# Attention, max-of-three and gated feed-forward on one core: last product's splits and sums moved to VectorE, its loads issued earlier, wo's sums in four steps in a row

## The chip, the cores and the metric

One core of a Trainium2 chip runs the whole program. The metric is the device time of one execution in microseconds; the median of the runs counts. TensorE is called PE in the rows, VectorE DVE, ScalarE ACT, GpSimd POOL, and SyncE, whose queue issues the DMAs, SP.

## What is computed

```python
scores = cap * tanh(q @ k.T / sqrt(64) / cap)        # 4 batches, 12 heads, 448 tokens, 64 wide
x   = softmax(scores) @ v                            # put together: 1792 tokens x 768
h   = maximum(maximum(x @ w1, x @ w2), x @ w3)       # 768 x 768 each
y   = h @ moe_w_out                                  # 1792 x 768
g   = silu(y @ w_gate) * (y @ w_val)                 # 1792 x 1536
out = g @ moe2_w_out                                 # 1792 x 768, float32
```

The weights arrive as 64-bit floats and are turned into float32 on the chip.

## The kernel before, in words

Every float32 matrix product is done in three: an operand is split into a high part (a copy that TensorE reads at full rate) and a low part (the operand less the high part), and high x high, high x low and low x high are summed in PSUM. Splitting (`parts_of`, L549 to L554) takes ScalarE one copy (L551) and another engine one subtraction (L554).

The change touches the end of the program. Gate and value come from 12 stages, c = 0 to 11 (`NF2`), each for 128 columns of both weights. A stage holds 14 products (`product`, L914 to L955): seven products of sums and differences in the manner of Strassen, in place of eight, for each of two token halves, p = 0 and 1. Its weights' seven operands (names o, made of A11, S3, S1, S2, A12, S4, A22) are cut in the stage before (`ops_steps`, L807 to L842): sums on GpSimd (L827), high parts on ScalarE, low parts on VectorE and two on GpSimd. VectorE adds each product's PSUM bank to tiles ct, qn and kn (L936 to L953; there are eight banks), ScalarE takes the silu (L947, L954), GpSimd multiplies (L950, L955), and the result goes to DRAM, to gd, by a store (`store`, L902 to L904). Stores wait in a list; a product sends all but the newest.

In between, the next weights are converted step by step (`convert`, L509 to L546): L527 on ScalarE, L531 to L538 on VectorE, L541 on GpSimd. Their tiles raw have two buffers. In stages 2 to 7 each stage also sums a piece of the last weight, wo, which lies converted in DRAM (wod): `sums_of_wo` (L490 to L507) loads it into a raw buffer, makes four differences on VectorE (L496), the fourth followed by a store to wsd (L500). These are four steps, at products 7, 9, 11 and 13 of the stage.

The last product, g by wo, is again of seven products, over pairs r of token blocks of 128 (7 pairs, gr holds what is loaded of gd; A11 and A12 are the two halves of a pair's first block, A21 and A22 of its second). `part` (L1045 to L1082) is one product of 18 matmuls; its list `todo` takes pairs 0 and 1 in turn, product by product, then pairs 2 to 6 one after another. `cut(i)` makes the operand of part i: a sum of blocks for S3 and S2 on VectorE, for S1 and S4 on GpSimd (L1026), then two half splits, the first half's low part on VectorE, the second's on GpSimd (`half_ops`, L958). It stands four parts ahead of its part. `split_wo` splits wo's 21 pieces (wo0 to wo20, three for each of the seven products), every third on GpSimd, and `fetch_wo` then loads the piece three further on; they share three buffers. Stage 11 takes the second token half first, since pairs 0 and 1 lie there.

Nothing is scheduled by a planner: each engine takes its instructions in the order in which the code issues them, and waits at the first one that is not ready. SP does likewise with loads and stores. The steps hang on the products of a stage in the table `at`.

Of the kernel before, what the change touches and what calls it, by code (L numbers as in the profile page):

```python
# [10 lines left out]
F32R = mybir.dt.float32r  # L11
# [3 lines left out]
ALU = mybir.AluOpType  # L15
# [93 lines left out]
def program(ctx, tc, tensors, shared, general):  # L109

    nc = tc.nc
# [6 lines left out]
    P = 128  # L118
# [533 lines left out]
    with tc.manual_schedule():  # L652
# [249 lines left out]
        def store():  # L902
            dst, src = stores.pop(0)
            nc.sync.dma_start(out=dst, in_=src)  # L904
# [9 lines left out]
        def product(c, p, n):  # L914
# [5 lines left out]
            for kk in range(3):  # L920
                k3 = slice(kk * P, (kk + 1) * P)
                for j, (s0, s1) in enumerate(((0, 0), (0, 1), (1, 0))):
# [1 line left out]
                        ps, a[:, s0, k3], m[:, kk, s1],  # L924
                        start=kk == 0 and j == 0, stop=kk == 2 and j == 2,
                    )
            while len(stores) > 1:
                store()
            add = nc.vector.tensor_add
            t = tmp.setdefault((c, p), {})  # L930
# [24 lines left out]
                nc.gpsimd.tensor_tensor(t[2], t[2], t[1], op=ALU.mult)  # L955
                stores.append((gd[:, c, (2 * p + 1) * S : (2 * p + 2) * S], t[2]))

        half_ops = (nc.vector, nc.gpsimd)  # L958
        OPS = "A11 S3 S1 S2 A12 S4 A22".split()
        WITH = "B11 T3 T1 T2 B21 B22 T4".split()  # L960
        flat0 = yo0.rearrange("p n k x s -> p (n k x s)")
# [22 lines left out]
        def split_wo():  # L984
            i = done_pieces[1]
            if i < len(pieces):
                done_pieces[1] += 1
                x, k = pieces[i]
                t = wo_c[x][:, k : k + 2]
                parts_of(t[:, :, 0], t[:, :, 1], wot.pop(i), nc.scalar, half_ops[i % 3 == 2])  # L990
                fetch_wo()

        blocks = [*range(T // P // 2, T // P), *range(T // P // 2)]
# [14 lines left out]
        def fetch_g(r, half=None):  # L1008
            c = slice(0, NF2) if half is None else slice(half * NHALF, (half + 1) * NHALF)
            for x in range(2):  # L1010
                s = blocks[2 * r + x]
                nc.sync.dma_start(out=gr[r, x][:, c], in_=gd[:, c, s * P : (s + 1) * P])

        def cut(i):
            if i >= len(todo):
                return
            r, n = todo[i]
            a11, a12, a21, a22 = (
                gr[r, x][:, y * NHALF : (y + 1) * NHALF].rearrange("p c t -> p (c t)")
                for x in range(2)  # L1020
                for y in range(2)
            )
            ve, pool_ = nc.vector, nc.gpsimd

            def add(eng, out_, x0, x1, op=ALU.subtract):
                eng.tensor_tensor(out_, x0, x1, op=op)  # L1026
                return out_

            x = OPS[n]
            if x == "S3":  # L1030
                src = add(ve, a11, a11, a21)
            elif x == "S1":
                src = add(pool_, a21, a21, a22, ALU.add)
            elif x == "S2":
                src = add(ve, a11, a22, a11)
            elif x == "S4":
                src = add(pool_, a12, a12, a11)
            else:
                src = dict(A11=a11, A12=a12, A22=a22)[x]
            for y in range(2):  # L1040
                t = wp.tile([P, 2, HW], F32R, tag="w", name=f"g{r}_{x}_{y}")
                parts_of(t[:, 0], t[:, 1], src[:, y * HW : (y + 1) * HW], nc.scalar, half_ops[y])
                ga.setdefault((r, n), []).append(t)

        def part(r, n):  # L1045
# [52 lines left out]
        for c in range(NF2):  # L1098
            at = {}
            if c + 1 < NF2:  # L1100
                for i in (0, 1, 2, 3, 3, 4, 5, 6) if c else (2, 3, 4, 5):
                    at.setdefault(i, []).append(convert_part)
                if 0 <= c + 1 - SUMS_AT < NHALF:
                    for i in (7, 9, 11, 13):
                        at.setdefault(i, []).append(convert_part)
                for i, step in enumerate(ops_steps(c + 1)):
                    at.setdefault(7 + i, []).append(step)
            both = [(n, p) for n in range(7) for p in range(2)]
            if c == 0:
                both.sort(key=lambda x: x[1])  # L1110
                for i, step in enumerate(y_steps):
                    at.setdefault(i, []).insert(0, step)
                at.setdefault(6, []).append(open_ct)
            if c == NF2 - 1:
                both.sort(key=lambda x: -x[1])
                at.setdefault(6, []).append(open_wo)
                at.setdefault(0, []).append(lambda: (open_g(0), fetch_g(0, 0)))
                for i in range(3):
                    at.setdefault(2 + i, []).append(fetch_wo)
                at.setdefault(8, []).append(lambda: ([store() for _ in [*stores]], cut(0)))  # L1120
                for i in (7, 7, 8, 9, 10, 11, 13):
                    at.setdefault(i, []).append(split_wo)
                at.setdefault(9, []).append(lambda: (fetch_g(0, 1), open_g(1), fetch_g(1, 0)))
                at.setdefault(10, []).append(lambda: (fetch_g(1, 1), cut(1)))
                at.setdefault(12, []).append(lambda: cut(2))
            for i, (n, p) in enumerate(both):
                product(c, p, n)
                for step in at.get(i, ()):
                    step()
# [3 lines left out]
        while stores:  # L1133
            store()
        cut(3)
        for i, (r, n) in enumerate(todo):
            part(r, n)
            if r < 2:
                split_wo()
                if i % 2:  # L1140
                    split_wo()
            cut(i + 4)
            if i + 4 < len(todo) and todo[i + 4][1] == 6 and todo[i + 4][0] + 2 < NPR:
                open_g(todo[i + 4][0] + 2)
                fetch_g(todo[i + 4][0] + 2)
# [25 lines left out]
```

## Time and profile before

| | before |
|---|---|
| median of 3 runs | 1103.56 us (1102.81 to 1104.5) |
| the profiled execution | 1102.74 us, of it span 1100.9 us |
| TensorE matmul busy | 1056.5 us, 96% of the span |
| VectorE busy | 762.0 us, 69% |
| GpSimd busy | 704.9 us, 64% |
| ScalarE busy | 535.9 us, 49% |
| mean granted TensorE clock | 0.987 |
| stages 0 to 11 | 614.5 to 923.8 us of the span |
| last product | from 923.8 us |

The span is the trace's own time from first to last instruction. Busy time says which engine has most work, not which one is waited for: that is read from the timeline, where a bracket behind a row gives the engine's idle time before it and what ended it. The granted clock is TensorE's as a share of full speed.

### The profile page before, as it was taken

To read this page: it belongs to the slowest core of one execution; us is meant where nothing else is said; L and a number is where in the kernel's file an instruction comes from. 1 tells how busy PE (TensorE), PEld (TensorE's weight loads), DVE (VectorE), ACT (ScalarE), POOL (GpSimd) and SP (SyncE) were. 2 spreads that over 40 slices of the span, in tenths; PEclk is the share of its full clock that TensorE was granted. 3 is DMA by queue.
4 is the path that set the end of the run, shared out by engine and by line. 5 is a ranking of instruction groups with operands and counts; after the bars stand their busy time and mean duration, and the time that the engine had idled before them with its cause. 6 is when DMAs were issued, how large, how long until landed. Compare 5 with 4: busy or idle time off the path is not lost. (4 is left out here: it accounts for less than half of the span.)

```text
span 1100.9 us, 15124 instructions
## 1 busy us (share of the span) xinstructions
PE 1056.5 (96%) x5354; PEld 914.8 (83%) x5354; DVE 762.0 (69%) x986; ACT 535.9 (49%) x842; POOL 704.9 (64%) x586
## 2 busy tenths in 40 slices
PE   8987999999999999999999999999999998799998
PEld 5533778888888888999998999999888998689998
DVE  4666898957777678767446977777777774675543
ACT  6855668867766674344435533222222333433321
POOL 1355998787887779998354356555555663676542
PEclk9989899999999999999999999999999998999999
DMA  6655445433434423433322023444443337473411
GB/s 150 164 143 127 116 112 149 119 92 113 135 99 117 123 70 121 136 119 114 100 71 83 9 83 120 149 149 148 148 149 120 108 96 232 131 223 107 130 65 40
DMA packets 165077, 131.42 MB, mean 119 GB/s; under 512 B 72832, under 2 KB 159616, under 8 KB 164992
## 3 DMA queue, kind: packets, MB, share of 16 engines
q1 hardware_dynamic: 162992, 129.91, 39.7%
q8 instruction: 44, 0.72, 0.3%
q10 hardware_dynamic: 2000, 0.46, 0.2%
q14 instruction: 41, 0.34, 0.1%
HBM read 98.70 MB, written 31.54 MB: 118 GB/s over the span
## 5 line engine op out<-in xcount | busy, mean ns | idle before, releaser
L600 PE MATMUL ps_h<-x,ws 128*128 128x448 f32 x1296 | 287.9, 368 | 0.5 <-DVE ht L626 0.5
L600 PEld LDWEIGHTS ps_h<-x,ws 128*128 128x128 f32 x1296 | 239.0, 188 | 35.2 <-issue 18.0
L554 POOL TENSOR_TENSOR ws<-w,ws 128x384 fp32r<-128x384 f32 x144 | 179.9, 1258 | 12.9 <-ACT ws L551 5.3
L541 POOL TENSOR_TENSOR t<-t,raw 128x768 uint32<-128x768 uint32 x42 | 82.9, 1974 | 114.2 <-DVE raw L538 104.6
L259 DVE TENSOR_TENSOR el<-e,eh 128x896 fp32r<-128x896 f32 x64 | 87.4, 1368 | 43.0 <-ACT eh L258 34.4
L241 ACT ACTIVATE e<-sc,four 128x896 f32<-128x896 f32 x96 | 87.2, 908 | 32.9 <-PE sc L235 32.7
L249 ACT ACTIVATE e<-e,four 128x896 f32<-128x896 f32 x96 | 99.5, 1037 | 0.8
L923 PE MATMUL ps_g<-yo,o_S 128*128 128x448 f32 x432 | 95.2, 364 | 4.5 <-DVE ct L943 3.4
L600 PE MATMUL ps_y<-ha,ws 128*128 128x448 f32 x432 | 89.4, 368 | 3.4 <-DVE ha L554 1.4
L923 PEld LDWEIGHTS ps_g<-yo,o_S 128*128 128x128 f32 x432 | 80.3, 187 | 13.0 <-DVE ct L943 4.5
L600 PEld LDWEIGHTS ps_y<-ha,ws 128*128 128x128 f32 x432 | 82.1, 191 | 10.7 <-DVE ha L554 2.0
L284 PE MATMUL pv<-eh,vs 128*128 128x448 f32 (+1 forms) x256 | 76.6, 380 | 1.4 <-POOL vs L185 1.4
L553 POOL TENSOR_SCALAR ws<-w 128x384 fp32r<-128x384 f32 x90 | 76.5, 850 | 0.0
L923 PE MATMUL ps_g<-yo,o_A 128*128 128x448 f32 x324 | 70.3, 362 | 0.0
L551 ACT ACTIVATE g_S<-gr 128x384 fp32r<-128x384 f32 x56 | 26.3, 517 | 81.1 <-POOL gr L1026 42.1
L527 ACT ACTIVATE t<-raw 128x768 f32<-128x768 f32 x42 | 37.6, 895 | 56.8 <-DMA raw<-in_moe_w_val_dram 46.3
L923 PEld LDWEIGHTS ps_g<-yo,o_A 128*128 128x128 f32 x324 | 60.7, 187 | 4.1
L531 DVE TENSOR_SCALAR t<-t 128x768 f32<-128x768 f32 x42 | 35.8, 853 | 37.2 <-ACT t L527 37.2
L554 POOL TENSOR_TENSOR g_S<-gr,g_S 128x384 fp32r<-128x384 f32 x28 | 28.7, 1025 | 51.2 <-ACT g_S L551 49.0
L284 PE MATMUL pv<-e,vp 128*128 128x448 f32 (+1 forms) x128 | 54.1, 608 | 5.9 <-DMA vp<-in_v_dram 4.4
L541 POOL TENSOR_TENSOR w<-w,raw 128x768 uint32<-128x768 uint32 x18 | 36.2, 2014 | 32.9 <-DVE raw L538 32.9
L258 ACT ACTIVATE eh<-e 128x896 fp32r<-128x896 f32 x64 | 55.0, 860 | 2.6 <-ACT e L249 0.6
(156 smaller groups left out, 2239.3 us busy)
## 6 DMA issues: line engine op xcount, KB each, us to landing
raw<-in_moe_w_dram SPq DMA_DIRECT2D x18, 768.0 KB, 4.9
raw<-in_moe_w_out_dram SPq DMA_DIRECT2D x18, 768.0 KB, 4.8
raw<-in_moe_w_gate_dram SPq DMA_DIRECT2D x12, 768.0 KB, 4.8
raw<-in_moe_w_val_dram SPq DMA_DIRECT2D x12, 768.0 KB, 4.5
gr<-gd SPq DMA_DIRECT2D x10, 768.0 KB, 6.9
rb<-rd SPq DMA_DIRECT2D x48, 112.0 KB, 3.1
h<-ht SPq DMA_DIRECT2D x24, 224.0 KB, 2.0
hr<-h SPq DMA_DIRECT2D x24, 224.0 KB, 2.8
```

What stands on the lines that cost most here:

```text
L241: nc.scalar.activation(ee[n][:, :w], ps[:, :w, :S], AF.Tanh, scale=qsc)
L249: nc.scalar.activation(t, t, AF.Exp, bias=ncap, scale=acap)
L258: nc.scalar.activation(hi, t, AF.Copy)
L259: nc.vector.tensor_sub(lo, t, f(hi))
L284: nc.tensor.matmul(pv[g][j][:, :S], a, m, start=c == 0 and x == 0, stop=c == 3 and x == len(ops) - 1,)
L527: nc.scalar.activation(f(t), high.bitcast(F32), AF.Abs)
L531: nc.vector.tensor_scalar(f(t), f(t), F64_LEAST, F64_MOST, ALU.max, ALU.min)
L541: nc.gpsimd.tensor_tensor(t, t, low, op=ALU.add)
L553: copier.tensor_scalar(hi, src, 1.0, 1.0, ALU.mult, ALU.mult)
L554: subtracter.tensor_tensor(lo, src, f(hi), op=ALU.subtract)
L600: nc.tensor.matmul(ps, a, m, start=kk == 0 and n == 0, stop=kk == NK - 1 and n == 2)
L923: nc.tensor.matmul(ps, a[:, s0, k3], m[:, kk, s1], start=kk == 0 and j == 0, stop=kk == 2 and j == 2,)
```

## The change

Four things are changed. The steps of wo's sums in stages 2 to 7 hang on products 7, 8, 9 and 10. In the last product all half splits, all wo pieces and all sums are VectorE's; the sums are no longer made in `cut` but in `pre`, which is issued one product earlier. The first load of pair 0 (its first column half) moves from stage 11 to product 7 of stage 10, the first of pair 1 from product 9 to product 6 of stage 11, and the loads of the second halves follow at products 8 and 9. From stage 10 on up to four stores may wait in the list, until product 8 of stage 11 sends them all.

```diff
-            while len(stores) > 1:
+            while len(stores) > (1 if c < NF2 - 2 else 4):
                 store()
...
-        half_ops = (nc.vector, nc.gpsimd)
...
-                parts_of(t[:, :, 0], t[:, :, 1], wot.pop(i), nc.scalar, half_ops[i % 3 == 2])
+                parts_of(t[:, :, 0], t[:, :, 1], wot.pop(i), nc.scalar, nc.vector)
...
+        PLACE = dict(A11=0, S3=0, S1=2, S2=0, A12=1, S4=1, A22=3)
+        MADE = dict(S3=(0, 2), S1=(2, 3), S2=(3, 0), S4=(1, 0))
+
+        def pre(i):
+            if i < len(todo) and OPS[todo[i][1]] in MADE:
+                r, n = todo[i]
+                a, x = blocks_of(r), OPS[n]
+                x0, x1 = MADE[x]
+                op = ALU.add if x == "S1" else ALU.subtract
+                nc.vector.tensor_tensor(a[PLACE[x]], a[x0], a[x1], op=op)
...
-            x = OPS[n]
-            if x == "S3":
-                src = add(ve, a11, a11, a21)
-            elif x == "S1":
-                src = add(pool_, a21, a21, a22, ALU.add)
-            elif x == "S2":
-                src = add(ve, a11, a22, a11)
-            elif x == "S4":
-                src = add(pool_, a12, a12, a11)
-            else:
-                src = dict(A11=a11, A12=a12, A22=a22)[x]
+            src = blocks_of(r)[PLACE[OPS[n]]]
...
-                parts_of(t[:, 0], t[:, 1], src[:, y * HW : (y + 1) * HW], nc.scalar, half_ops[y])
+                parts_of(t[:, 0], t[:, 1], src[:, y * HW : (y + 1) * HW], nc.scalar, nc.vector)
...
-                    for i in (7, 9, 11, 13):
+                    for i in (7, 8, 9, 10):
                         at.setdefault(i, []).append(convert_part)
...
-                at.setdefault(0, []).append(lambda: (open_g(0), fetch_g(0, 0)))
...
-                at.setdefault(8, []).append(lambda: ([store() for _ in [*stores]], cut(0)))
+                at.setdefault(6, []).append(lambda: (open_g(1), fetch_g(1, 0)))
+                at.setdefault(8, []).append(lambda: ([store() for _ in [*stores]], fetch_g(0, 1)))
+                at.setdefault(9, []).append(lambda: fetch_g(1, 1))
...
-                at.setdefault(9, []).append(lambda: (fetch_g(0, 1), open_g(1), fetch_g(1, 0)))
-                at.setdefault(10, []).append(lambda: (fetch_g(1, 1), cut(1)))
-                at.setdefault(12, []).append(lambda: cut(2))
+                at.setdefault(8, []).append(lambda: cut(0))
+                at.setdefault(10, []).append(lambda: (cut(1), pre(2)))
+                at.setdefault(12, []).append(lambda: (cut(2), pre(3)))
+            if c == NF2 - 2:
+                at.setdefault(7, []).append(lambda: (open_g(0), fetch_g(0, 0)))
...
         cut(3)
+        pre(4)
         for i, (r, n) in enumerate(todo):
...
             cut(i + 4)
+            pre(i + 5)
```

What this does to the order of the instructions is seen at three places. The first is VectorE's queue in the second half of stage 7 (raw119 is the piece of wo that is summed, L554 are low parts of stage 8's weights, L946 to L953 the additions of products). Before:

```order
L554 TENSOR_TENSOR o8_S3_7754<-t94_7647,o8_S3_7754 128x384
L946 TENSOR_TENSOR ct7_1_0_7661<-ps_g7_1_4_7773,ct7_1_0_7661 128x448
L496 TENSOR_TENSOR raw119_7694<-raw119_7694 128x384
L949 TENSOR_TENSOR kn0_62<-ps_g7_0_5_7790,kn0_62 128x448
L554 TENSOR_TENSOR o8_S2_7753<-t94_7647,o8_S2_7753 128x384
L949 TENSOR_TENSOR kn1_63<-ps_g7_1_5_7806,kn1_63 128x448
L496 TENSOR_TENSOR raw119_7694<-raw119_7694 128x384
L554 TENSOR_TENSOR o8_A12_7804<-t94_7647,o8_A12_7804 128x384
L953 TENSOR_TENSOR ct7_0_1_7675<-ps_g7_0_6_7823,ct7_0_1_7675 128x448
L554 TENSOR_TENSOR o8_A22_7805<-t95_7692,o8_A22_7805 128x384
L953 TENSOR_TENSOR ct7_1_1_7689<-ps_g7_1_6_7839,ct7_1_1_7689 128x448
L496 TENSOR_TENSOR raw119_7694<-raw119_7694 128x384
```

And of the change:

```order
L496 TENSOR_TENSOR raw119_7694<-raw119_7694 128x384
L554 TENSOR_TENSOR o8_S3_7754<-t94_7647,o8_S3_7754 128x384
L946 TENSOR_TENSOR ct7_1_0_7661<-ps_g7_1_4_7774,ct7_1_0_7661 128x448
L496 TENSOR_TENSOR raw119_7694<-raw119_7694 128x384
L949 TENSOR_TENSOR kn0_62<-ps_g7_0_5_7791,kn0_62 128x448
L496 TENSOR_TENSOR raw119_7694<-raw119_7694 128x384
L554 TENSOR_TENSOR o8_S2_7753<-t94_7647,o8_S2_7753 128x384
L949 TENSOR_TENSOR kn1_63<-ps_g7_1_5_7809,kn1_63 128x448
L554 TENSOR_TENSOR o8_A12_7807<-t94_7647,o8_A12_7807 128x384
L953 TENSOR_TENSOR ct7_0_1_7675<-ps_g7_0_6_7825,ct7_0_1_7675 128x448
L554 TENSOR_TENSOR o8_A22_7808<-t95_7692,o8_A22_7808 128x384
L953 TENSOR_TENSOR ct7_1_1_7689<-ps_g7_1_6_7841,ct7_1_1_7689 128x448
```

The second sum of wo (the first L496 of the first list) now stands ahead of the S3 split, and the fourth, which stood behind everything, ahead of the S2 split; before both lists the first sum stands at the same place.

The second place is SP's queue in stage 11, from the load of wo3 on before and from the store of qn0 (stage 10's) on in the change (kn1 and ct11_1_2 hold stage 11's results of the second token half). Before:

```order
L982 DMA wo3_8629<-wsd_192 128x2x384
L982 DMA wo4_8633<-wsd_192 128x2x384
L904 DMA gd_6065<-ct11_1_2_8559 128x448
L982 DMA wo5_8656<-wsd_192 128x2x384
L982 DMA wo6_8671<-wsd_192 128x2x384
L1012 DMA gr0_0_8520<-gd_6065 128x6x128
L1012 DMA gr0_1_8521<-gd_6065 128x6x128
L1012 DMA gr1_0_8675<-gd_6065 128x6x128
L1012 DMA gr1_1_8676<-gd_6065 128x6x128
L982 DMA wo7_8694<-wsd_192 128x2x384
L1012 DMA gr1_0_8675<-gd_6065 128x6x128
L1012 DMA gr1_1_8676<-gd_6065 128x6x128
```

And of the change:

```order
L904 DMA gd_6065<-qn0_60 128x448
L1011 DMA gr1_0_8611<-gd_6065 128x6x128
L1011 DMA gr1_1_8612<-gd_6065 128x6x128
L904 DMA gd_6065<-qn1_61 128x448
L981 DMA wo3_8630<-wsd_192 128x2x384
L981 DMA wo4_8634<-wsd_192 128x2x384
L904 DMA gd_6065<-ct10_0_2_8387 128x448
L904 DMA gd_6065<-ct10_1_2_8401 128x448
L904 DMA gd_6065<-kn1_63 128x448
L904 DMA gd_6065<-ct11_1_2_8556 128x448
L1011 DMA gr0_0_8410<-gd_6065 128x6x128
L1011 DMA gr0_1_8411<-gd_6065 128x6x128
```

Pair 1's first load (gr1) moves ahead of wo3; four stores now stand behind wo4, directly ahead of pair 0's second load. Pair 0's first load stands further up, right behind the load of the last value weights, and two stores of stage 9 behind it.

The third is VectorE's queue in the last product, about the additions of pair 0's and pair 1's fourth part (S2). Before:

```order
L554 TENSOR_TENSOR yo0_5339<-wo15_8888,yo0_5339 128x2x384
L554 TENSOR_TENSOR g1_A12_0_8953<-gr1_0_8675,g1_A12_0_8953 128x384
L1070 TENSOR_TENSOR o0_1_8978<-ps_o0_3_8959,o0_0_8784 128x384
L1071 TENSOR_TENSOR o0_2_8980<-ps_o0_1_8833,o0_1_8978 128x384
L1072 TENSOR_TENSOR o0_1_8978<-ps_o0_2_8897,o0_1_8978 128x384
L1073 TENSOR_TENSOR o0_3_8983<-ps_o0_2_8897,o0_2_8980 128x384
L554 TENSOR_TENSOR yo0_5339<-wo16_8918,yo0_5339 128x2x384
L554 TENSOR_TENSOR g0_S4_0_8991<-gr0_0_8520,g0_S4_0_8991 128x384
L1070 TENSOR_TENSOR o1_1_9016<-ps_o1_3_8997,o1_0_8816 128x384
L1071 TENSOR_TENSOR o1_2_9018<-ps_o1_1_8863,o1_1_9016 128x384
L1072 TENSOR_TENSOR o1_1_9016<-ps_o1_2_8926,o1_1_9016 128x384
L1073 TENSOR_TENSOR o1_3_9021<-ps_o1_2_8926,o1_2_9018 128x384
```

And of the change:

```order
L1029 TENSOR_TENSOR gr0_0_8410<-gr0_0_8410 128x768
L1066 TENSOR_TENSOR o0_1_8979<-ps_o0_3_8960,o0_0_8785 128x384
L1067 TENSOR_TENSOR o0_2_8981<-ps_o0_1_8834,o0_1_8979 128x384
L1068 TENSOR_TENSOR o0_1_8979<-ps_o0_2_8897,o0_1_8979 128x384
L1069 TENSOR_TENSOR o0_3_8984<-ps_o0_2_8897,o0_2_8981 128x384
L554 TENSOR_TENSOR yo0_5339<-wo16_8918,yo0_5339 128x2x384
L554 TENSOR_TENSOR g0_S4_0_8991<-gr0_0_8410,g0_S4_0_8991 128x384
L554 TENSOR_TENSOR g0_S4_1_8994<-gr0_0_8410,g0_S4_1_8994 128x384
L1029 TENSOR_TENSOR gr1_0_8611<-gr1_0_8611 128x768
L1066 TENSOR_TENSOR o1_1_9017<-ps_o1_3_8998,o1_0_8817 128x384
L1067 TENSOR_TENSOR o1_2_9019<-ps_o1_1_8864,o1_1_9017 128x384
L1068 TENSOR_TENSOR o1_1_9017<-ps_o1_2_8926,o1_1_9017 128x384
```

Each operand's second half and the sums (L1029, which were GpSimd's here) are now in VectorE's queue, between the two groups of four additions.

## Rows read from the trace of the kernel before

**Rows 1.** TensorE's timeline (start us, us, engine, line, instruction, count, [idle before, releaser]).

```profile
614.53 1.96 PE L923 MATMUL ps_g<-yo,o_A 128*128 128x448 f32 x9
...
785.90 1.96 PE L923 MATMUL ps_g<-yo1c,o_A 128*128 128x448 f32 x9
789.02 2.08 PE L923 MATMUL ps_g<-yo,o_S 128*128 128x448 f32 x9 [1.16 <-DVE ct L943]
...
898.62 1.96 PE L923 MATMUL ps_g<-b,o_A 128*128 128x448 f32 x9
```

**Rows 2.** Timeline of all engines, in stage 7.

```profile
790.73 0.55 DVE L496 TENSOR_TENSOR raw<-raw 128x384 f32<-128x384 f32 x1
...
803.59 0.54 DVE L496 TENSOR_TENSOR raw<-raw 128x384 f32<-128x384 f32 x1
...
804.16 0.32 SPq L500 DMA_DIRECT2D wsd<-raw  x1
...
807.52 0.38 SPq L482 DMA_DIRECT2D raw<-in_moe_w_val_dram  x1
...
812.00 0.89 ACT L527 ACTIVATE t<-raw 128x768 f32<-128x768 f32 x1 [5.66 <-DMA raw<-in_moe_w_val_dram]
...
813.00 0.56 DVE L531 TENSOR_SCALAR t<-t 128x768 f32<-128x768 f32 x1 [2.56 <-ACT t L527]
...
818.31 0.55 DVE L496 TENSOR_TENSOR raw<-raw 128x384 f32<-128x384 f32 x1
```

**Rows 3.** TensorE's timeline in the last product.

```profile
923.82 3.29 PE L1052 MATMUL ps_o<-wo,g_A 128*128 128x384 f32 x18
930.12 6.07 PE L1052 MATMUL ps_o<-wo,g_A 128*128 128x384 f32 x18 [3.01 <-ACT g_A L551]
936.02 3.28 PE L1052 MATMUL ps_o<-wo,g_S 128*128 128x384 f32 x18
...
950.63 3.64 PE L1052 MATMUL ps_o<-wo,g_S 128*128 128x384 f32 x18 [1.89 <-ACT g_S L551]
...
985.78 3.28 PE L1052 MATMUL ps_o<-wo,g_A 128*128 128x384 f32 x18
988.90 3.29 PE L1052 MATMUL ps_o<-wo,g_S 128*128 128x384 f32 x18
992.40 3.64 PE L1052 MATMUL ps_o<-wo,g_S 128*128 128x384 f32 x18 [0.21 <-ACT g_S L551]
```

**Rows 4.** Busy time by stretches; the last three columns: granted clock, DMA share, GB/s.

```profile
925.00:930.00 5.00, 2.11 (x13) 1.79 (x11) 0.00 (x0) 0.46 (x2) 0.00 (x0) 0.91 1.18 308
930.00:935.00 5.00, 4.88 (x15) 4.79 (x16) 4.25 (x6) 2.73 (x6) 3.40 (x3) 0.50 0.73 190
...
950.00:955.00 5.00, 4.11 (x20) 3.32 (x20) 3.13 (x4) 2.72 (x6) 1.08 (x3) 1.00 0.44 132
```

**Rows 5.** Timelines of VectorE and GpSimd in the last product.

```profile
936.79 0.96 DVE L554 TENSOR_TENSOR wo<-wo,wo 128x768 fp32r<-128x768 f32 x1 [1.38 <-ACT wo L551]
936.81 1.96 POOL L955 TENSOR_TENSOR ct<-ct,ct 128x448 f32<-128x448 f32 x1
937.66 1.92 DVE L1026 TENSOR_TENSOR gr<-gr,gr 128x768 f32<-128x768 f32 x1
...
967.48 0.55 DVE L1070 TENSOR_TENSOR o<-ps_o,o 128x384 f32<-128x384 f32 x1
```

**Rows 6.** Instructions on tiles g_S and gr (count: ns min/median/max).

```profile
L554 DVE TENSOR_TENSOR g_S<-gr,g_S x28: 545/559/1636, 933.2 to 1082.1; 128x384 fp32r<-128x384 f32 x28
L554 POOL TENSOR_TENSOR g_S<-gr,g_S x28: 1014/1025/1052, 935.8 to 1082.7; 128x384 fp32r<-128x384 f32 x28
...
L1026 POOL TENSOR_TENSOR gr<-gr x14: 1832/1851/2524, 941.7 to 1079.7; 128x768 f32<-128x768 f32 x14
```

**Rows 7.** DMA issues from 895 to 990 us (count, KB each, median us to landing).

```profile
gr<-gd SPq DMA_DIRECT2D x8, 384.0 KB, 6.4
gr<-gd SPq DMA_DIRECT2D x4, 768.0 KB, 7.5
```

More of the change, by code (lines that the diff above doesn't have):

```diff
@@ L1012, in fetch_g, with blocks_of @@
                 nc.sync.dma_start(out=gr[r, x][:, c], in_=gd[:, c, s * P : (s + 1) * P])
+        def blocks_of(r):
+            return [
+                gr[r, x][:, y * NHALF : (y + 1) * NHALF].rearrange("p c t -> p (c t)")
+                for x in range(2)
+                for y in range(2)
+            ]
+        PLACE = dict(A11=0, S3=0, S1=2, S2=0, A12=1, S4=1, A22=3)
[7 more added lines that the diff above has]
+                nc.vector.tensor_tensor(a[PLACE[x]], a[x0], a[x1], op=op)
         def cut(i):
@@ L1017, in cut @@
             r, n = todo[i]
[L1018 to L1027, printed above, removed]
-            x = OPS[n]
-            if x == "S3":
-                src = add(ve, a11, a11, a21)
-            elif x == "S1":
-                src = add(pool_, a21, a21, a22, ALU.add)
-            elif x == "S2":
-                src = add(ve, a11, a22, a11)
-            elif x == "S4":
-                src = add(pool_, a12, a12, a11)
-            else:
-                src = dict(A11=a11, A12=a12, A22=a22)[x]
+            src = blocks_of(r)[PLACE[OPS[n]]]
             for y in range(2):
-                t = wp.tile([P, 2, HW], F32R, tag="w", name=f"g{r}_{x}_{y}")
-                parts_of(t[:, 0], t[:, 1], src[:, y * HW : (y + 1) * HW], nc.scalar, half_ops[y])
+                t = wp.tile([P, 2, HW], F32R, tag="w", name=f"g{r}_{OPS[n]}_{y}")
+                parts_of(t[:, 0], t[:, 1], src[:, y * HW : (y + 1) * HW], nc.scalar, nc.vector)
                 ga.setdefault((r, n), []).append(t)
```

## The prediction

> **What bounds the kernel now.** Read first the busy shares and the TensorE timeline. In the gate and value stages (c = 0 to 11) TensorE has 14 products a stage, one every 1.80 us, so 25.2 us a stage. From the first product of stage 0 to the first of stage 11 [rows 1] lie 898.62 - 614.53 = 284.09 us, and 11 stages need 277.2: 6.9 us are lost. In TensorE's whole timeline the gaps stand only from 771 to 853 us (an example is the jump from 785.90 to 789.02 [rows 1], 3.12 instead of 1.80). VectorE makes them: in the stages with wo's sums its own period is 818.31 - 790.73 = 27.58 us [rows 2], 2.4 more than TensorE's. TensorE's lead over it (up to eight PSUM banks) is eaten over the first stages, and the rest is lost.
>
> Why 27.58? Read the chain in [rows 2] downwards. The fourth sum is VectorE's at 803.59, only then the store of the sums goes out (804.16), its buffer comes free when that has landed (the load of the next value weights issues at 807.52, 3.36 later), ScalarE gets the weights at 812.00, and VectorE, in order, has sat idle 2.56 us for it until 813.00.
>
> In the last product a part (18 matmuls) takes 988.90 - 985.78 = 3.12 us when nothing waits [rows 3]. The first two pairs of token blocks, interleaved, are 14 parts, 43.7 us; they take 985.78 - 923.82 = 61.96, so 18.3 too many. Of that, part two starts at 930.12 instead of 926.94 (3.2, for the load of pair 1) and then runs to 936.02, 5.90 instead of 3.12: the granted clock stands at 0.50, the lower level of 1.2 GHz, after TensorE had idled 3.01 us [rows 3, 4]. That is 2.8 more. The other 12.3 are waits of 0.2 to 1.9 us (one is at 950.63) behind sums and splits. Pair 2's second part loses another 0.4 (988.90 to 992.40 is 3.50). From 992.40 to the end TensorE never waits. So at most 6.9 + 18.3 + 0.4 = 25.6 us can be had.
>
> GpSimd is why the sums and splits are late. A sum takes it 1.85 us and a half split 1.03; VectorE's half split takes 0.56 [rows 6] and its split of a wo piece 0.96 [rows 5]. And the two shut each other out: GpSimd's product begun at 936.81 ends at 938.77, and VectorE's sum begun at 937.66 ends only at 939.58, 0.81 after it [rows 5].
>
> **The change, part by part.** Durations are those of the profiled execution, 1102.74 us (span 1100.9); the median of the runs, 1103.56, is 0.8 above it.
>
> *Sums in four steps in a row, stages 2 to 7.* The fourth sum moves ahead of the S2 split, some 7 us earlier in VectorE's queue. Its store then lands well before ScalarE wants the value weights, and the 2.56 us idle shrinks to some 0.5, since ScalarE's copy must still wait for the gate's: about -2.1. The second sum now stands before the S3 split, whose copy VectorE waited for anyway. Against this: sums two and four now meet GpSimd's subtractions of 1.0 us, and by [rows 5] wait for them. I put +0.4 for the S3 split, and the S2 split comes some 2.3 later; it is wanted two products into the next stage, with 3.9 us to spare when VectorE has no lag. VectorE's period becomes 27.6 - 2.1 = 25.5 us. Over six stages it falls behind by 6 x 0.3 = 1.8 us. The old run shows what lag is free: 6 x 2.4 = 14.3 were run up and 6.9 lost, so 7.4 cost nothing. The whole **6.9** comes back; the ends are 0 (no shorter period) and 6.9. The Trainium skill's "SBUF — State Buffer" (Who interferes with whom) says that a VectorE instruction with two SBUF inputs and a GpSimd one that reads SBUF lock each other out for a whole instruction, which speaks against sums beside GpSimd's; [rows 5] agree. By it the period is the 25.5 above, and without a lock some 24.9; both lie under the 26.4 (25.2 + 6.9 / 6) from which a loss would be left over.
>
> *Earlier loads, stores held back.* The first halves of pair 0 load in stage 10, of pair 1 as soon as TensorE is done with the second token half: 923.82 - 7 x 1.80 = 911.2. (Times here are on the old clock; the 6.9 shifts all alike.) With 6.4 us to landing [rows 7] it is there at 918. ScalarE comes to it behind two wo pieces at 921, VectorE ends the splits at 924.0, and TensorE wants them at 926.94: the 3.2 and the 2.8 go. The price is in the queue: two stores of stage 9 go out after the new loads, some 12 us late, from buffers that are written again only after 911; four more wait until 917. Pair 0's second halves therefore issue at about 920.2, not 921.3, behind the last store's landing, and are there at 926.6; they are wanted by the S1 sum at 933.9. So I cost the holding back at nothing, with 7 us of cover.
>
> *Splits and sums on VectorE alone.* In the 14 parts VectorE then holds 28 half splits (0.56), 14 wo pieces and 8 sums (0.96 each) and 14 additions (0.55) [rows 5, 6]: 15.7 + 21.1 + 7.7 = 44.5 us. Neighbours overlap by some 0.08 us (936.79 to 937.66 is 0.87, the first lasts 0.96 [rows 5]), so 64 instructions take about 39.4 of TensorE's 43.7. It fits, barely. GpSimd's four sums, 14 half splits and five wo pieces (as large as a sum), 7.4 + 14.4 + 9.3 = 31 us of mutual lock, are gone.
>
> Walking its queue in order: sum S3 of pair 0 from 923.9, wo5 (its load lands at 925 to 928) split by 927.8, both halves by 929.3, and TensorE wants it at 930.06. Pair 1's S3 has its first half at 933.5, wanted at 933.18: 0.3. Then one part follows another: S1 936.7 and 940.3, S2 943.0 and 946.6, A12 948.4 and 951.9, wanted at 936.5, 939.6, 942.8, 945.9, 949.0 and 952.1; the first half is ready half a microsecond before these ends, so all told 0.1. The pinch is S4: four additions in a row (2.1), wo16, then S4's first half at 956.3, wanted at 955.2: 0.8. Four more additions, then wo17 at 960.5, wanted two thirds into that part, at 958.05: 2.4. After it VectorE is ahead again. Together 3.6, so pair 2 starts at 923.82 + 43.7 + 3.6 = 971.1.
>
> Pair 2's loads issue when pair 0's A22 is split, 963.3 and 964.8 in the walk. At 7.5 us [rows 7] they land by 972.3 at the latest; the second is wanted for S3, split by 974.4, and TensorE wants it at 974.2. I add 0.3: 971.4. Before it was 985.78: 14.4, and the 0.4 in pair 2 goes as well: **14.8**. In the later pairs VectorE has 14 half splits, four sums and seven additions, some 14 us of 21.8; no cost.
>
> *The sum.* 6.9 + 14.8 = 21.7; 1102.74 - 21.7 = 1081.0, on the median's footing **1081.9 us**. Nothing else is touched: the rest of the order is the same.
>
> **Rivals.**
> *The clock falls again.* The longest wait left in the walk is 2.4 us. After 3.01 us idle the clock fell [rows 3, 4]; after the 1.89 before 950.63 it stayed at 1.00 [rows 3, 4]. If it falls, 2.8 more: 1084.7.
>
> *The stages stay VectorE's.* If the sums lose to GpSimd what the store's earlier landing gains, the period stays near 27.5 and the 6.9 is not had: 1088.8. For it speaks that both moved sums stand beside GpSimd's work; against it that the 2.56 us are a pure wait for a load.
>
> *The loads land late.* The DMA engines are full at 925 to 930 (share 1.18 [rows 4]), and the change puts four stores, four half loads and three wo pieces into 917 to 924. A wo5 at 6.5 us or more would put S3 back by 2 to 3 us, and TensorE would idle and drop its clock once more: 3 + 2.8, so 1087.7.
>
> *Slower.* The next pair's first sum now stands a part earlier in VectorE's in-order queue, ahead of this pair's additions. If a pair's load had not landed by then, all of VectorE, and through the additions TensorE's banks, would stop. To lose more than 21.7 us, each of five pairs would have to stop 4.4 us, with loads landing over 20 us after issue; they take 7.5 and are issued a pair (21.8 us) ahead. Then 1106.
>
> *It does not do what it says.* If TensorE's gaps came from something else than GpSimd's and the loads' lateness, no change: 1103.6. The idle rows name both.
>
> **How the numbers follow.** The forecast (1077.5 to 1084) 0.56, clock 0.14, stages 0.12, late loads 0.12, slower 0.03, none 0.03. The upper bound of the gain, 25.6, gives 1078.0 at best; I put the low end at 1077. The high end, 1091, takes in the late loads and the unrecovered stages with 2 us to spare, as neither excludes a part of the other. Left out are both in full, slower and none, and some of the stages' case: under 2 in 10. A measurement of this kernel tells 0.2%, 2.2 us, from no change; faster is all but the last two and their neighbours: 0.94, same 0.03, slower 0.03.
>
> **What would show it.** Right: stage 11's first product near 891.7, no gap in TensorE's rows from 771 to 853, the first sums of the stages nearer to 25.2 than 27.5 us apart; no wait and no half clock at the second part of the last product; pair 2 some 47 to 48 us after the last product's start, not 62; no GpSimd splits there; the longest wait at S4 behind VectorE. Wrong: gaps in the stages that end with S2's split or the additions; a part of 5.9 us; a wait that ends with a load of gr or wo.

## The result, and the profile after

The changed kernel takes 1085.01 us (median of 4 runs, 1083.36 to 1086.47) against 1103.18 of the kernel before in the same comparison: ratio 0.9834 [0.9814, 0.9853], 18.2 us less. Forecast were 1081.9 us and a gain of 21.7. The time lies in the range (1077 to 1091) and a microsecond beyond the likeliest case's own range (1077.5 to 1084). The execution profiled took 1085.95 us, its span is 1084.2. Run once more (below) the same kernel takes 1084.8 us, ratio 0.9857 [0.9838, 0.9877], 15.8 us less: so the gain is known to some 2 us.

TensorE's timeline of the changed kernel, the first products of stages 0 and 11 and two of stage 7, which answer to [rows 1]:

```profile
616.18 1.96 PE L923 MATMUL ps_g<-yo,o_A 128*128 128x448 f32 x9
...
785.38 1.96 PE L923 MATMUL ps_g<-yo,o_A 128*128 128x448 f32 x9
787.18 1.96 PE L923 MATMUL ps_g<-yo1c,o_A 128*128 128x448 f32 x9
...
893.38 1.96 PE L923 MATMUL ps_g<-b,o_A 128*128 128x448 f32 x9
```

893.38 - 616.18 = 277.20 us: exactly the 11 x 25.2 that TensorE needs. No row between them, shown or left out, has a bracket, so all 6.9 us of the stages are back. Rows of VectorE, ScalarE and SP in stage 7, from all engines' timeline, which answer to [rows 2] (789.27 is the fourth sum):

```profile
783.41 0.55 DVE L496 TENSOR_TENSOR raw<-raw 128x384 f32<-128x384 f32 x1
...
789.27 1.10 DVE L496 TENSOR_TENSOR raw<-raw 128x384 f32<-128x384 f32 x1
...
790.39 0.34 SPq L500 DMA_DIRECT2D wsd<-raw  x1
...
796.63 0.43 SPq L482 DMA_DIRECT2D raw<-in_moe_w_val_dram  x1
...
801.63 0.92 ACT L527 ACTIVATE t<-raw 128x768 f32<-128x768 f32 x1 [3.21 <-DMA raw<-in_moe_w_val_dram]
...
802.66 1.18 DVE L531 TENSOR_SCALAR t<-t 128x768 f32<-128x768 f32 x1
...
808.66 0.55 DVE L496 TENSOR_TENSOR raw<-raw 128x384 f32<-128x384 f32 x1
```

The store now goes out 7.0 us after the stage's first sum instead of 13.4 [rows 2], and 6.2 us before the load of the value weights issues (796.63), not 3.4. ScalarE still waits for that load; VectorE, whose 2.56 us of idle time stood here, does not (the row at 802.66 has no bracket). First sums lie 808.66 - 783.41 = 25.25 us apart, which is TensorE's pace.

TensorE's timeline in the last product, which answers to [rows 3] (a bracket is the idle time before, with what ended it):

```profile
918.58 6.40 PE L1048 MATMUL ps_o<-wo,g_A 128*128 128x384 f32 x36
924.82 0.53 PE L1048 MATMUL ps_o<-wo,g_S 128*128 128x384 f32 x2
926.31 3.05 PE L1048 MATMUL ps_o<-wo,g_S 128*128 128x384 f32 x16 [0.96 <-DVE g_S L554]
930.90 0.61 PE L1048 MATMUL ps_o<-wo,g_S 128*128 128x384 f32 x2 [1.54 <-ACT g_S L551]
932.25 9.29 PE L1048 MATMUL ps_o<-wo,g_S 128*128 128x384 f32 x52 [0.73 <-DVE g_S L554]
941.37 6.40 PE L1048 MATMUL ps_o<-yo,g_S 128*128 128x384 f32 x36
...
954.94 2.18 PE L1048 MATMUL ps_o<-yo,g_S 128*128 128x384 f32 x11 [0.57 <-DVE g_S L554]
959.25 4.38 PE L1048 MATMUL ps_o<-yo,g_S 128*128 128x384 f32 x23 [2.14 <-DVE yo L554]
...
969.71 3.28 PE L1048 MATMUL ps_o<-wo,g_A 128*128 128x384 f32 x18
972.83 6.65 PE L1048 MATMUL ps_o<-wo,g_S 128*128 128x384 f32 x36
```

The first row holds parts one and two without a break: the wait of 3.01 us and the part at half clock of [rows 3] are gone. From 918.58 to pair 2 at 969.71 are 51.13 us, before 61.96 [rows 3]; 14 parts need 43.7. The 7.45 us that are left stand in two places. From 918.58 to 941.37 are 22.79 us for six parts (A11, S3 and S1 of both pairs, 108 matmuls, 18.72 us): **4.07 us lost at S3**. From there to 969.71 are 28.34 us for eight parts (24.96): **3.38 lost at S4** (the waits, and what the matmuls after them take longer). The forecast put the first at 0.4 at most and the second at 3.2.

Why S3 is late, in SP's, ScalarE's and VectorE's timelines about the last product's start (918.58):

```profile
911.61 0.94 SPq L904 DMA_DIRECT2D gd<-ct  x2
912.65 0.40 SPq L904 DMA_DIRECT2D gd<-kn  x1
913.45 0.34 SPq L904 DMA_DIRECT2D gd<-ct  x1
916.78 0.96 SPq L1011 DMA_DIRECT2D gr<-gd  x2
917.84 0.49 SPq L981 DMA_DIRECT2D wo<-wsd  x1
...
923.42 0.85 ACT L551 ACTIVATE wo<-wo 128x768 fp32r<-128x768 f32 x1 [2.88 <-DMA wo<-wsd]
...
924.30 0.96 DVE L554 TENSOR_TENSOR wo<-wo,wo 128x768 fp32r<-128x768 f32 x1 [4.37 <-ACT wo L551]
```

Pair 0's second halves (916.78) read what kn1's store (912.65) wrote, so SP waits for its landing, 4.1 us; behind them in the same queue stands the load of wo5, which S3 needs. It issues only 0.7 us before the last product begins, ScalarE waits for it until 923.42, and VectorE, in order, stands idle for 4.37 us.

Busy time by stretches (the columns are length, busy time of PE, PEld, DVE, ACT, POOL; then granted clock, DMA share, GB/s) shows the idle VectorE, full DMA engines (1.10), and the full clock behind both losses:

```profile
920.00:925.00 5.00, 5.00 (x30) 4.93 (x29) 0.70 (x1) 2.12 (x4) 0.00 (x0) 1.00 1.10 311
925.00:930.00 5.00, 3.39 (x18) 2.75 (x17) 4.09 (x6) 0.97 (x3) 1.56 (x2) 1.00 0.64 207
930.00:935.00 5.00, 3.37 (x18) 3.05 (x19) 4.53 (x7) 3.75 (x9) 0.91 (x1) 1.00 0.35 104
...
955.00:960.00 5.00, 2.86 (x15) 2.54 (x16) 4.93 (x9) 2.61 (x5) 0.00 (x0) 1.00 0.42 119
```

S4 is the pinch that was forecast. VectorE's timeline there:

```profile
953.46 0.95 DVE L554 TENSOR_TENSOR yo<-wo,yo 128x768 fp32r<-128x768 f32 x1
954.33 1.02 DVE L554 TENSOR_TENSOR g_S<-gr,g_S 128x384 fp32r<-128x384 f32 x2
955.27 0.95 DVE L1029 TENSOR_TENSOR gr<-gr 128x768 f32<-128x768 f32 x1
956.13 0.55 DVE L1066 TENSOR_TENSOR o<-ps_o,o 128x384 f32<-128x384 f32 x1
...
958.25 1.82 DVE L554 TENSOR_TENSOR yo<-wo,yo 128x768 fp32r<-128x768 f32 x2
```

It never rests here; S4's last wo piece (wo17) is begun at 958.25, behind pair 1's four additions, and TensorE waits 2.14 us for it. GpSimd has no work left in the last product once stage 11's results are done (0.00 in the stretch from 955), and VectorE's sum takes 0.95 us here, not the 1.92 beside GpSimd's work [rows 5].

The ledger of the two profiled executions: stages 6.9, last product to pair 2 10.8 (61.96 - 51.13), from pair 2 to the end of the span 0.6 (115.1 to 114.5), less 1.65 because stage 0 began at 616.18 instead of 614.53: 16.7 = 1100.9 - 1084.2. Nothing ahead of stage 0 was changed; in the runs below it begins anywhere from 611.2 to 615.1, so those 1.65 us are the run's.

### The profile page after: what moved, and what is told of

Its sections match the earlier page's. It is cut to its first block, busy times and chain, and to the rows that moved or that the text cites. A ratio compares the mean times of both kernels' runs of the same rounds, so it can differ in the third digit from the quotient of the medians.

```text
span 1084.2 us, 15089 instructions
## 1 busy us (share of the span) xinstructions
PE 1049.0 (97%) x5354; PEld 913.1 (84%) x5354; DVE 784.1 (72%) x1056; ACT 538.1 (50%) x842; POOL 613.0 (57%) x516
## 5 line engine op out<-in xcount | busy, mean ns | idle before, releaser
L554 POOL TENSOR_TENSOR ws<-w,ws 128x384 fp32r<-128x384 f32 x144 | 182.5, 1276 | 15.2 <-ACT ws L551 7.7
L259 DVE TENSOR_TENSOR el<-e,eh 128x896 fp32r<-128x896 f32 x64 | 84.7, 1325 | 47.1 <-ACT eh L258 41.8
L947 ACT ACTIVATE ct<-ct 128x448 f32<-128x448 f32 x23 | 13.3, 579 | 92.0 <-DVE ct L946 92.0
L235 PEld LDWEIGHTS sc<-qh,kh 64*128 64x128 f32 (+1 forms) x168 | 18.3, 187 | 40.2 <-issue 18.5
```

The costliest lines, as they stand in the source:

```text
L259: nc.vector.tensor_sub(lo, t, f(hi))
L554: subtracter.tensor_tensor(lo, src, f(hi), op=ALU.subtract)
```

## The experiments

Three questions: does each part give what it was priced at, what makes S3 late, and can S3 and S4 be mended? Each kernel has one trace; stages, window and losses are of that one execution. The table gives for each kernel the median with its ratio to the kernel before on the same chip, the time from stage 0's first product to the last product's start (TensorE needs 302.4), and the time from there to pair 2, the *window* (43.7 needed), both read from TensorE's timeline. For some of them the loss in the window is split as above.

| kernel | median, us | ratio to before | stages | window | lost at S3 | at S4 |
|---|---|---|---|---|---|---|
| before | 1103.18 | | 309.29 | 61.96 | | |
| changed | 1085.01 | 0.9834 [0.9814, 0.9853] | 302.40 | 51.13 | 4.07 | 3.38 |
| changed, once more | 1084.8 | 0.9857 [0.9838, 0.9877] | 302.40 | 51.28 | 4.33 | 3.27 |
| wo's sums alone | 1094.03 | 0.9937 [0.9918, 0.9956] | 302.41 | 61.88 | | |
| loads and stores alone | 1099.61 | 0.9987 [0.9973, 1.0] | 309.83 | 59.35 | | |
| VectorE alone | 1093.84 | 0.9936 [0.9922, 0.9949] | 309.67 | 55.51 | | |
| sums not ahead | 1090.16 | 0.9888 [0.9867, 0.9908] | 302.40 | 59.80 | | |
| half the splits on GpSimd | 1086.05 | 0.9859 [0.984, 0.9878] | 302.40 | 51.73 | | |
| wo5 first | 1081.57 | 0.9824 [0.9809, 0.9839] | 302.41 | 50.21 | 1.77 | 4.76 |
| stores at once | 1081.71 | 0.9814 [0.9794, 0.9835] | 302.40 | 49.90 | 1.16 | 5.06 |
| wo5 first, wo17 sooner | 1079.9 | 0.9806 [0.9787, 0.9826] | 302.40 | 48.22 | 1.82 | 2.72 |
| stores at once, wo17 sooner | 1080.86 | 0.981 [0.979, 0.9829] | 302.40 | 48.27 | 1.65 | 2.94 |
| all three | 1080.6 | 0.9807 [0.9791, 0.9822] | 302.41 | 47.91 | 1.55 | 2.68 |

### One part at a time

**wo's sums alone**: the kernel before with one line.

```diff
-                    for i in (7, 9, 11, 13):
+                    for i in (7, 8, 9, 10):
```

> Only the steps of wo's sums are moved. Theory: VectorE's period in stages 2 to 7 is what costs TensorE 6.9 us there, and the earlier store of the sums shortens it below what the PSUM banks absorb. Then some 6.9 us less than before (about 1096.3 against 1103.2), stages 0 to 11 at 25.2 us each, and the last product as before (62 us to pair 2). Rival (the stages recovered through the held stores or through something else in the change): no change, 1103, and gaps in TensorE's rows between 771 and 853 us.

By the ratio 6.9 us less (0.0063 of 1101.25), the stages take 302.41 and the window is the old one. The first term of the sum stands by itself, at its full size.

**Loads and stores alone**: GpSimd keeps its splits and sums.

```diff
-            while len(stores) > 1:
+            while len(stores) > (1 if c < NF2 - 2 else 4):
...
+                at.setdefault(6, []).append(lambda: (open_g(1), fetch_g(1, 0)))
+                at.setdefault(8, []).append(lambda: ([store() for _ in [*stores]], fetch_g(0, 1)))
+                at.setdefault(9, []).append(lambda: fetch_g(1, 1))
...
+                at.setdefault(7, []).append(lambda: (open_g(0), fetch_g(0, 0)))
```

> Only the loads move and the stores are held back; GpSimd keeps its splits and sums. Theory: pair 1's late load costs 3.2 us of waiting and 2.8 us of half clock, so the second part of the last product starts on time at full clock; GpSimd's splits and sums then keep the later parts late and may take back a part. 4 to 6 us less, 1097 to 1099. Rival (splits and sums set the pace anyway, the load is hidden behind them): under 1.5 us, above 1101.7.

A miss: 1.4 us less by the ratio, where the early load was priced at 6.0. Rows of TensorE's timeline, then of ScalarE and VectorE from all engines' timeline:

```profile
921.02 6.40 PE L1052 MATMUL ps_o<-wo,g_A 128*128 128x384 f32 x36
...
934.90 8.44 PE L1052 MATMUL ps_o<-wo,g_S 128*128 128x384 f32 x36 [1.86 <-ACT g_S L551]
945.23 4.95 PE L1052 MATMUL ps_o<-wo,g_S 128*128 128x384 f32 x18 [1.89 <-ACT g_S L551]
```

```profile
926.38 0.84 ACT L551 ACTIVATE wo<-wo 128x768 fp32r<-128x768 f32 x1 [4.08 <-DMA wo<-wsd]
...
927.66 1.86 DVE L554 TENSOR_TENSOR g_S<-gr,g_S 128x384 fp32r<-128x384 f32 x1 [4.58 <-ACT g_S L551]
...
944.65 0.94 ACT L551 ACTIVATE g_S<-gr 128x384 fp32r<-128x384 f32 x2 [3.70 <-POOL gr L1026]
```

The second part is on time (the first row holds both), but TensorE then runs into the next waits, and rows of 8.44 us for 36 matmuls (6.40 at full clock) and 4.95 for 18 (3.28) show that the clock falls there instead (granted clock 0.66 from 935 to 940 and from 945 to 950). Two things stand behind the early load. S1 comes no sooner than GpSimd makes its sum (944.65). And the held stores make wo5 late in this kernel too: its load issues at 920.18, behind that of pair 0's second halves (919.13), which waits for kn1's store; ScalarE gets it at 926.38, 5.36 us after the last product's start, S3's copies stand behind it, and VectorE idles 4.58 us for them. No run has the early loads without the held stores and with GpSimd's splits and sums, so how much of the miss is wo5's and how much GpSimd's stays open.

**VectorE alone**: splits, wo pieces and sums on VectorE, a product ahead; loads, stores and stages as before.

```diff
-                parts_of(t[:, 0], t[:, 1], src[:, y * HW : (y + 1) * HW], nc.scalar, half_ops[y])
+                parts_of(t[:, 0], t[:, 1], src[:, y * HW : (y + 1) * HW], nc.scalar, nc.vector)
...
+            pre(i + 5)
```

> Only the splits and sums of the last product move to VectorE, the sums a product ahead; loads, stores and wo's sums as before. Theory: the 6.0 us of the late load and half clock stay, the 12.3 us of waits behind sums and splits fall to about 4 to 7 us (S4 alone 3.4): 5 to 8 us less, 1095 to 1098. Rival (VectorE becomes the bound and gives back what it takes): 1101 to 1106.

7.1 us less by the ratio, the window 6.45 shorter, with the wait for pair 1's load (2.77 us) still in it. With these splits the loads and held stores are worth 55.51 - 51.13 = 4.4 us of window; alone they were worth 2.6. The three parts give 6.9 + 1.4 + 7.1 = 15.4 singly; together they give 18.2, or 15.8 in the repeat, so that the times do not show more than the sum of the parts. Of the window it is 2.6 + 6.5 = 9.1 singly and 10.8 together.

**Sums not ahead**: the changed kernel with each sum made inside `cut`.

```diff
+            pre(i)
             src = blocks_of(r)[PLACE[OPS[n]]]
...
-            pre(i + 5)
```

> The changed kernel with each sum made directly before its copy and split, not a product ahead. Theory: VectorE then idles from each sum to the end of ScalarE's copy, 0.6 us for each of eight sums, in a window in which it is nearly full: 2 to 4 us more than the changed kernel, and rows of VectorE that wait 0.6 us for g_S. Rival (operands are cut four parts ahead, so the idle time is hidden): within 1 us of it.

More than expected: the window is 59.80, 8.7 longer, and the time 3.4 to 5.9 us longer (against the changed kernel's two ratios; the execution traced is the slowest of the four, 1093.22). TensorE waits at six of the eight S parts, and the clock falls twice, to 0.66 from 932 to 937 and from 966 to 971. TensorE's timeline, the first fall:

```profile
926.42 0.62 PE L1049 MATMUL ps_o<-wo,g_S 128*128 128x384 f32 x2 [2.57 <-ACT g_S L551]
...
932.39 8.06 PE L1049 MATMUL ps_o<-wo,g_S 128*128 128x384 f32 x36 [2.13 <-ACT g_S L551]
```

Both waits end with ScalarE: made in `cut`, a sum is followed at once by ScalarE's copy of it and by VectorE's subtraction of that copy, and VectorE idles between (0.7 us in these two places). At the first, the sum also stands behind wo5's late split in VectorE's queue and is made at 924.80, 7.4 us after the last product's start; in the changed kernel it is made 0.1 us before that start (918.44), ahead of the split.

**Half the splits on GpSimd**: the changed kernel, each operand's second half back on GpSimd.

```diff
-                parts_of(t[:, 0], t[:, 1], src[:, y * HW : (y + 1) * HW], nc.scalar, nc.vector)
+                parts_of(t[:, 0], t[:, 1], src[:, y * HW : (y + 1) * HW], nc.scalar, (nc.vector, nc.gpsimd)[y])
```

> The changed kernel with every second half split of the last product back on GpSimd; sums and wo pieces stay with VectorE. Theory: GpSimd's 14 splits of 1.03 us in the first two pairs lock VectorE out and come later than VectorE's own would: 2 to 6 us more than the changed kernel, and VectorE's instructions beside them stretched. Rival (only GpSimd's sums of 1.85 us and wo pieces were in the way; the half splits relieve a nearly full VectorE): the same or up to 3 us less.

The rival came true: 0.9859 cannot be told from the changed kernel's 0.9857, and the 2.8 us to its 0.9834 lie within the intervals; the window is 0.5 longer. GpSimd and VectorE here, from all engines' timeline:

```profile
939.44 1.09 POOL L554 TENSOR_TENSOR g_S<-gr,g_S 128x384 fp32r<-128x384 f32 x1 [2.42 <-ACT g_S L551]
939.57 1.78 DVE L1029 TENSOR_TENSOR gr<-gr,gr 128x768 f32<-128x768 f32 x1
```

VectorE's sum takes 1.78 us beside GpSimd's half split and 0.95 without. The Trainium skill's "SBUF — State Buffer" (Who interferes with whom) has a VectorE instruction with two SBUF inputs and a GpSimd one that reads SBUF lock each other out, and these rows agree. But the lock costs the program little here: VectorE has 52 instructions in the window instead of 64 and is busy for 42.17 us instead of 41.78, so it loses to the lock about what it is spared. That GpSimd's half splits went too was not shown to be worth anything; what pays is the sums and wo pieces on VectorE and the sums a product ahead, taken together. How much of it is the engine's and how much the order's is not shown: sums left on GpSimd but made a product ahead were not tried, nor the wo pieces by themselves.

### What makes S3 late

**wo5 first**: the changed kernel, wo5's load moved ahead of the held stores and pair 0's second halves, wo6's only ahead of pair 1's second halves.

```diff
+                for i in (7, 7, 8, 9, 10, 11, 13):
+                    at.setdefault(i, []).append(split_wo)
                 at.setdefault(8, []).append(lambda: ([store() for _ in [*stores]], fetch_g(0, 1)))
                 at.setdefault(9, []).append(lambda: fetch_g(1, 1))
-                for i in (7, 7, 8, 9, 10, 11, 13):
-                    at.setdefault(i, []).append(split_wo)
```

> The changed kernel, with the loads of wo5 and wo6 issued ahead of the stores and of the second halves of pairs 0 and 1. Theory: the 4.1 us that TensorE loses about S3 hang on the load of wo5, which issues at 917.84 in the changed kernel and lands 5.5 us later while the DMA engines are full; issued at 912.6 it is there at 917, and S3 starts on time: 3 to 4 us less than the changed kernel's 1085.0, about 1081.5. Rival (S3 waits for VectorE's queue: additions, silu, sums): under 1 us less, 1084 or more.

The loss at S3 falls from 4.07 to 1.77, the wait there to 0.60. But the loss at S4 rises from 3.38 to 4.76 with the very same wait. TensorE's timeline and the stretch:

```profile
928.09 10.05 PE L1048 MATMUL ps_o<-wo,g_S 128*128 128x384 f32 x52 [0.60 <-DVE g_S L554]
...
955.79 5.83 PE L1048 MATMUL ps_o<-yo,g_S 128*128 128x384 f32 x23 [2.14 <-DVE yo L554]
```

```profile
955.00:960.00 5.00, 4.21 (x15) 4.21 (x16) 5.00 (x9) 1.62 (x4) 0.00 (x0) 0.66 0.54 161
```

After 2.14 us of idle the same 23 matmuls take 5.83 us instead of 4.38, at a granted clock of 0.66 over the stretch. So the window is only 0.92 us shorter, and the 3 to 4 us that were expected did not come in the time: 0.9824 cannot be told from 0.9834.

**Stores at once**: the changed kernel, stores no longer held back, wo5 behind the second halves as in the change.

```diff
-            while len(stores) > (1 if c < NF2 - 2 else 4):
+            while len(stores) > 1:
```

> The changed kernel without the holding back of stores (a product sends all but the newest, as before). Theory: the holding back is worth nothing either way, the stores lie beside other work: within 1 us of the changed kernel, 51 us from the last product's start to pair 2. Rival (the loads of wo or of pair 1 get stuck behind stores that wait for GpSimd, and that is what holding back avoids): 1 to 4 us more.

By the ratios this kernel is 2.2 us (within the intervals) to 4.7 us (clear of them) faster than the changed one, and its window is 1.2 us shorter, which the forecast's "costed at nothing" did not allow. SP's queue:

```profile
904.55 0.47 SPq L904 DMA_DIRECT2D gd<-kn  x1
907.65 1.23 SPq L981 DMA_DIRECT2D wo<-wsd  x2
...
909.49 1.22 SPq L1011 DMA_DIRECT2D gr<-gd  x2
910.81 0.65 SPq L981 DMA_DIRECT2D wo<-wsd  x1
```

kn1's store goes out at 904.55, ahead of wo3 and wo4, and has landed when the second halves come up. They issue 6.4 us before the last product's start (915.90) instead of 1.8, and wo5 5.1 before it instead of 0.7. S3 loses 1.16 us. (S4 again loses more, 5.06, with the clock down after a wait of 2.21.) So both edits, by different ways, show the same cause of the loss at S3: the held stores stand ahead of wo5. What either is worth in time is less sure, since S4 gave some of it back.

### What wo17 sooner does to S4

**wo5 first, wo17 sooner**: the kernel "wo5 first", and in the last product the next wo piece is split behind every even part instead of every odd one.

```diff
-                if i % 2:
+                if i % 2 == 0:
                     split_wo()
```

> The version with wo5 first, and in the last product the second wo piece is split at even parts, not at odd ones: wo17 then stands ahead of the second group of four additions. Theory: S4 waits for wo17 only because four additions and a sum stand before it in VectorE's queue; the 2.1 us wait goes, and with it the half clock that follows it: some 2 to 3.5 us less than with wo5 first, 48 us or less from the last product's start to pair 2. Rival (VectorE's work as a whole, 39 of 43.7 us, is the limit): the wait only moves to S4's first half or to another part, under 1 us.

TensorE's timeline:

```profile
949.27 3.39 PE L1048 MATMUL ps_o<-yo,g_S 128*128 128x384 f32 x18 [0.75 <-DVE g_S L554]
954.06 3.04 PE L1048 MATMUL ps_o<-yo,g_S 128*128 128x384 f32 x16 [1.40 <-DVE g_S L554]
```

wo17's wait of 2.14 us is gone and the clock stands at 1.00, but 0.75 and 1.40 stay behind S4's own halves. The window is 48.22, 2.0 shorter than with wo5 first. Most of that is the clock that did not fall (1.45); against the changed kernel, whose clock did not fall either, S4 loses only 0.66 less (2.72 against 3.38). So the wait has for the most part moved to the halves, as the rival has it: VectorE's rows there have no idle time between them, so its work as a whole is the limit. By the ratios the time is 2.0 us less than with wo5 first, which lies within the intervals.

**All three edits**, and **stores at once with wo17 sooner**:

> All that the runs so far found, together: stores sent at once, wo5 and wo6 loaded ahead of pair 0's second halves, and the next wo piece split after every even part, so that wo17 comes a part sooner. Theory (the last product's loss at S3 is the late wo5 and nothing else, that at S4 is wo17): wo5 is early by either of the two edits, so the second is worth nothing more, wo17's 2.1 us wait goes; the last product's start to pair 2 is 47 to 48.3 us, the time the same as with wo5 first and wo17 sooner, 1079 to 1081. Rival (each of the two edits buys its own 2 us, as the held stores also delay pair 0's second halves, which the S1 sum needs): window under 46.5 us, 1077.5 to 1078.5.

> The changed kernel with its stores sent at once and the next wo piece split after every even part; wo5's load stays behind pair 0's second halves. Theory (sending the stores at once already brings wo5 in time): the same as the kernel with all three edits, window 47 to 48.3 us, 1079 to 1081. Rival (wo5's place in SP's queue still costs with the stores sent early): a wait of 1 to 2 us at pair 0's S3 remains, window 49 to 50 us, 1081 to 1083.

Both as the theory has it, 47.91 and 48.27 us of window: wo5 need be early by one of the two ways, and the second adds nothing that can be measured.

**The changed kernel once more**, beside these two:

> The changed kernel itself, once more on this chip, so that the two others are compared with it in the same call. Both theories: 1084 to 1087 us, window 51 us with waits of some 4 us at S3 and 3.4 us at S4. If it came out under 1082 us, the gains of the last versions would be differences between chips.

1084.8 us: so the versions with wo17 sooner beat it by 4 us on the same chip, and the kernel before by some 21. They cannot be told from one another, nor by time from the kernel with the stores at once alone (0.9814), whose window is 1.6 us longer. The simplest of those with the shorter window is the one with the stores sent at once, as it needs two lines.

## Why the prediction was right or wrong

*Stages, 6.9.* Right in size and reason. The moved store takes away VectorE's wait. The fourth sum does meet GpSimd's work (1.10 us at 789.27, 0.54 at 803.59 before); the second and third met it before as well (1.06 and 0.97 before, 1.12 and 1.06 now). The period stays under what TensorE allows. The working left its own 0.4 for the S3 split out of the 25.5; with it 25.9, which still lies under the bound of 26.4 (that bound goes by the 7.4 us that cost nothing, not by the 6.9 that were lost). The changed kernel and the one-line kernel give 6.9 each; the rival that the stages stay VectorE's is out.

*The late load of pair 1, 3.2 + 2.8.* Right in this kernel: wait and half clock are gone. The run with the loads alone adds what the text did not say: together with the held stores, and nothing else, it is worth 1.4 us of time, since wo5, late through these stores, and GpSimd's lateness stood right behind it.

*Holding the stores back, "costed at nothing, with 7 us of cover".* **This is the step that failed**, inside a range that held. It looked at who waits for pair 0's second halves (the S1 sum, with 7 us to spare) and not at what stands behind them in SP's queue: wo5. It also had the second halves issue 3.6 us before the last product's start; they issue 1.8 before, as kn1's store goes out third of four and needs 4.1 us to land. The walk took wo5 to be landed 1.2 to 4.2 us after the start; ScalarE got it at 4.84.

*The walk through VectorE's queue, 3.6 us left over.* S3 and S1 were put at 0.4 and cost 4.07. With wo5 on time (the five kernels with either edit) 1.2 to 1.8 remain, so 2.3 to 2.9 belong to wo5. The rest has a place in the rows: the walk left out stage 11's last additions on VectorE and the silus that stand ahead of wo5 and wo6 in ScalarE's queue. With the stores at once (start 915.90), from ScalarE's and VectorE's timelines:

```profile
917.34 0.58 ACT L947 ACTIVATE ct<-ct 128x448 f32<-128x448 f32 x1 [3.46 <-DVE ct L946]
917.82 0.83 ACT L551 ACTIVATE wo<-wo 128x768 fp32r<-128x768 f32 x1
...
918.68 0.96 DVE L554 TENSOR_TENSOR wo<-wo,wo 128x768 fp32r<-128x768 f32 x1 [1.38 <-ACT wo L551]
```

wo5's copy has no wait for its load here, but it stands behind a silu that waits for VectorE's addition, and VectorE then idles 1.38 us for the copy. That this makes up all of the rest was not tried. S4 was right in size and place: 3.2 forecast, 3.38 measured, and wo17's wait 2.14 of the 2.4 forecast. That wo17's place in the queue is the reason was right only in part, since most of the wait comes back at S4's halves when wo17 is split sooner.

*Pair 2.* It starts 51.13 us after the last product's start, not 47.3; its own second part loses 0.25 instead of 0.3. From pair 2 on 0.6 us were gained, 0.1 forecast (0.4 less 0.3).

*The rivals.* "The loads land late" named the mechanism, wo5 coming late and S3 falling back by 2 to 3 us, and gave it 0.12; it came true without the fall of the clock that was added to it, and by the place in SP's queue, not by slow transfers alone. "The clock falls again" did not happen in the changed kernel, but did at the very wait it named in two of its variants, at 1.45 us (5.83 - 4.38) rather than 2.8. "Slower" and "none" are out.

So of 21.7 us forecast 18.2 came, and 15.8 in the repeat. In the traces the window is 3.8 us longer than forecast (51.13 against 47.3), of which 2.3 to 2.9 are the held stores, and 0.5 more than forecast came behind it.

## What to carry to other kernels

When a change holds transfers back or moves them, walk the whole in-order queue behind them, not only the readers of the data that is moved: here a load with 7 us of cover, waiting for a held store to land, delayed the weight piece right behind it, which had none. A gain read off the first wait of a chain is worth what the next wait leaves of it: the early load, with the stores held back, shortened the window by 2.6 us on the kernel before and by 4.4 once VectorE had the splits and sums. And in a walk through a queue, count what the stage before still has in it.

## What was not expected of the hardware

The same idle time of TensorE is followed by half clock in one run and by full clock in another. After 2.14 us before the 23 matmuls of S4 they take 4.38 us in the changed kernel (granted clock 1.00 from 955 to 960), and after the same 2.14 us 5.83 with wo5 first (0.66); in its repeat the changed kernel again kept the full clock after 2.13 us, and with the stores at once it fell after 2.21. Before the change it stayed at 1.00 after 1.89 us [rows 3, 4]; in the kernel with wo's sums alone it fell after 1.90 us in the same product:

```profile
943.00:948.00 5.00, 5.00 (x20) 4.71 (x20) 2.89 (x4) 2.78 (x6) 1.98 (x2) 0.66 0.31 98
```

At S3, waits of 1.54 and 0.72 us with VectorE alone were followed by half clock too (52 matmuls in 10.86 us), and the changed kernel's 1.54 and 0.73 were not (9.29). What decides between the two is open: no run varied it alone, and each edited kernel has one trace, so that it may differ from one execution of a kernel to the next. For pricing it means that a wait of about 2 us can cost 1.5 us on top, or nothing.
